# Re-ordering the first weight and input transfers of a fused linear-attention and MLP kernel

## The chip, the cores and the metric

The kernel runs on one core of a Trainium2 chip. The core has five engines that run side by side: TensorE (PE, matrix products and transposes), VectorE (DVE), ScalarE (ACT), GpSimd (POOL) and SyncE (SP, which here only issues DMAs). Sixteen DMA engines move data between memory and the core. The metric is the device time of one execution in microseconds; lower is better.

## The reference

Block-wise linear attention with a decay per head, and behind it a layer norm with a two-layer MLP and a residual:

```python
for b in range(nb):                        # blocks along the sequence, state carried
    intra = einsum('bhic,bhjc->bhij', qb, kb) * Dmask      # Dmask = lam**(i-j), lower triangle
    intra = einsum('bhij,bhjd->bhid', intra, vb)
    inter = einsum('bhid,bhde->bhie', qb * lam_pow, kv_state)
    out[:, :, sl] = intra + inter
    kv_state = lam_block * kv_state + einsum('bhsd,bhse->bhde', kb * rev_pow, vb)
...
xn = (x - mean(x)) / sqrt(var(x) + 1e-06) * g_ln
out = x + maximum(xn @ w_ch1, 0) @ w_ch2
```

q, k and v are 4 x 8 x 768 x 64 (batch, heads, sequence, head size), so x has 3072 rows of 512. w_ch1 is 512 x 2048, w_ch2 2048 x 512. All inputs and the output are float32.

## The kernel before

The 3072 rows are 24 tiles of 128 rows; six tiles make a batch entry, and the attention state runs from tile to tile inside it. For each tile `t` the attention is cut into steps:

- `load_tile(t)` puts three DMAs of 256 KB (k, q, v) on SP's queue. Six buffers of each exist, so tile `t` takes the buffer of tile `t - 6`.
- `p0(t)` issues the load of a later tile and calls `bf_inputs(t)`: POOL makes `kb` (a cast of k, L142), `qb` (q scaled, L144) and `vb` (v scaled, L146), all bf16.
- `p1(t)`: PE transposes `kb` into `tk` and `qb` into `tq`; ACT copies `tk` to `kTp` (two halves), ACT or DVE copies `tq` to `qT`.
- `p2(t)`: PE makes `pk` (the state's increment) and `sc` (the scores); DVE adds the old state (`Stmp`) and masks the scores (`mA`, two halves); POOL multiplies the state by its decay (`Sn`, L185). In the first tile of a batch entry DVE makes `Sn` itself with `lamC`.
- `p3(t)`: PE makes `po` from `mA`, `vb`, `qT` and the state; ACT copies it to `x`; DVE makes the statistics and `xc`.
- `p4(t)`: PE transposes `xc` into `xt`, ACT copies that to `xT` of the tile's group and makes `std`, DVE makes `rstd`.

The MLP works on groups of one to four tiles. For a group of n tiles, `m1(u)` is a unit of first-layer products (`pm`, L254) followed by a ReLU on ACT into `hT`; `m2(i, part)` is a unit of four second-layer products (L267) for tile `i`, and after its fourth part DVE makes `o` and SP stores it. Units with `w1` need the chunk of first-layer weights in question, and `m2(i, part)` needs chunk `part` of `w2`.

The weights come in eight chunks, `load_w1(0..3)` and `load_w2(0..3)`, each issued from POOL's queue with a cast to bf16 (512 KB written). POOL executes its instructions in the order written, so a DMA that POOL issues goes out when POOL has come to it. `load_tile(t, after_pool=True)` ties an SP load to that order: POOL writes one element of the k buffer (L63), and the k load waits for it; SP issues in order too, so all later loads wait behind it.

The order of all engines is the program's order (there is no scheduler). It has three parts: the opening (tiles 0 to 3 with their weights, then the first-layer units of groups 0 and 1), a list `units` with a table `after` that puts attention steps of tiles 4 to 10 between the MLP units of groups 0 to 3, and a loop over the units of the groups from 4 on. That loop spreads the remaining `steps` evenly: at each unit, `rate` is the largest number of steps per unit that any later group still needs (`upto(g)` counts the steps up to the `p4` of the group's last tile), and `pace` adds it up. `round_of(j)` gives the order of steps per round. The opening before, and the group sizes:

```python
sizes = [2, 2, 1, 1, 2, 3, 3, 4, 4, 2]
run((p1, 0), (p2, 0), (p0, 2), (p1, 1), (p3, 0), (p2, 1))
load_w1(0); load_w1(1)
run((p1, 2), (p3, 1)); p0(3); load_w1(2)
run((p2, 2), (p4, 0), (p1, 3), (p3, 2), (p2, 3), (p4, 1))
load_w1(3); load_tile(4, after_pool=True); load_w2(0..3); load_tile(5, after_pool=True)
```

In the text, w1(c) and w2(c) are weight chunks, k4, q4, v4 the inputs of tile 4, and m1a and m1b the first-layer units of groups 0 and 1 in four quarters each (0 to 3).

Of the kernel before, what the change touches and what calls it, by code (L numbers as in the profile page):

```python
# [8 lines left out]
BF16 = mybir.dt.bfloat16  # L9
# [7 lines left out]
def kernel(  # L17
# [11 lines left out]
    nc = tc.nc  # L29
    B, H, S, D = q.shape  # L30
    C = 128
    nb = S // C
    NT = B * nb
    DM = H * D
    DF = moe_w_ch1.shape[1]
    NP = H // 2
# [11 lines left out]
    wk = ctx.enter_context(tc.tile_pool(name="wk", bufs=3))  # L48
# [5 lines left out]
    qkv_in = {}  # L54

    def load_tile(t, after_pool=False):
        b, c = divmod(t, nb)
        got = {}
        for name, src in (("k", k), ("q", q), ("v", v)):
            f = inp.tile([128, H, D], F32, tag=name + "in", name=name + "in")  # L60
            if after_pool:

                nc.gpsimd.memset(f[:, 0, 0:1], 0.0)  # L63
                after_pool = False
            nc.sync.dma_start(f, src[b, :, c * C:(c + 1) * C, :].rearrange("h p d -> p h d"))
            got[name] = f
        qkv_in[t] = got
# [6 lines left out]
    def load_w1(c):  # L74
        nc.gpsimd.dma_start(w1[c], moe_w_ch1[:, c * W1C:(c + 1) * W1C].rearrange("(k p) f -> p k f", p=128))
# [34 lines left out]
    lamC = const.tile([128, NP, 128], F32)  # L110
# [13 lines left out]
    lam_c = const.tile([128, H], F32)  # L124
    nc.scalar.activation(lam_c, lnlam, ACT.Exp, scale=float(C))
    sqrt_first = const.tile([128, 1], F32)
    nc.scalar.activation(sqrt_first, eps_t, ACT.Sqrt)
    lam_cp = lam_c.rearrange("p (a two) -> p a two", two=2)
    nc.vector.tensor_copy(lamC[0:64, :, 0:64], lam_cp[0:64, :, 0:1].to_broadcast([64, NP, 64]))
    nc.vector.tensor_copy(lamC[64:128, :, 64:128], lam_cp[64:128, :, 1:2].to_broadcast([64, NP, 64]))  # L130


    st = {}
# [2 lines left out]
    mv_keep = {}  # L136
    xT_of = {}

    def bf_inputs(t):
        f = qkv_in.pop(t)  # L140
        kb = wk.tile([128, H, D], BF16, tag="kb", bufs=4, name="kb")
        nc.gpsimd.tensor_copy(kb, f["k"])  # L142
        qb = wk.tile([128, H, D], BF16, tag="qb", name="qb")
        nc.gpsimd.tensor_tensor(qb, f["q"], lam_q[:, :, None].to_broadcast([128, H, D]), op=ALU.mult)  # L144
        vb = wk.tile([128, H, D], BF16, tag="vb", bufs=4, name="vb")
        nc.gpsimd.tensor_tensor(vb, f["v"], lam_v[:, :, None].to_broadcast([128, H, D]), op=ALU.mult)  # L146
        st[t] = dict(qb=qb, kb=kb, vb=vb)

    def p1(t):
        s = st[t]  # L150
# [130 lines left out]

        return m1, m2

    sizes = [2, 2, 1, 1, 2, 3, 3, 4, 4, 2]
    groups = [list(range(sum(sizes[:i]), sum(sizes[:i + 1]))) for i in range(len(sizes))]
    assert groups[-1][-1] == NT - 1
    group_of = {t: g for g, ts in enumerate(groups) for t in ts}

    def p0(t):
        if t > 3 and t + 4 < NT:  # L290
            load_tile(t + 4)
        bf_inputs(t)


    def p3_p0(t):
        p3(t)
        if t + 3 < NT:
            p0(t + 3)

    def round_of(j):  # L300
        steps = [(p1, j), (p3_p0, j - 1), (p2, j), (p4, j - 2)]
        return [(f, t) for f, t in steps if t < NT]

    def run(*steps):
        for f, *a in steps:
            f(*a)


    p0(0)
    p0(1)  # L310
    run((p1, 0), (p2, 0), (p0, 2), (p1, 1), (p3, 0), (p2, 1))
    load_w1(0)
    load_w1(1)
    run((p1, 2), (p3, 1))
    p0(3)
    load_w1(2)
    run((p2, 2), (p4, 0), (p1, 3), (p3, 2), (p2, 3), (p4, 1))
    load_w1(3)
    load_tile(4, after_pool=True)
    for c in range(NWC):  # L320
        load_w2(c)
    load_tile(5, after_pool=True)
# [5 lines left out]
    def m1s(f, c):  # L328
        for u in range(c * m1a.count // NWC, (c + 1) * m1a.count // NWC):
            f(u)  # L330
# [3 lines left out]
    m1s(m1a, 1)  # L334
    p4(3)
    m1s(m1a, 2)
    p0(4)
    for c in range(3):
        m1s(m1b, c)
    m1s(m1a, 3)  # L340
# [14 lines left out]

    steps = []
    for j in range(8, NT + 2):
        steps += [s for s in round_of(j) if s not in ((p3_p0, 7), (p4, 7), (p4, 6))]

    def upto(g):  # L360
        return steps.index((p4, groups[g][-1])) + 1 if g < len(groups) else len(steps)
# [47 lines left out]
```

## Time and profile before

| | before |
|---|---|
| median of 3 runs | 247.38 us (247.32 to 247.84) |
| profiled execution, its own time | 246.76 us |
| profiled execution, span from first to last instruction | 245.0 us |
| PE busy | 219.0 us (89% of the span) |
| ACT / DVE / POOL busy | 121.1 / 112.9 / 92.9 us |
| mean granted TensorE clock | 0.986 of full speed |
| DMA traffic | 29.91 MB, mean 122 GB/s |

The profile is one execution on the chip. Each engine has its busy time and the idle time before each instruction, with the instruction or DMA that ended it. A PE that is busy may still run at half clock: the granted clock stands in a row of its own. Lines such as L144 are lines of the kernel before. The 1.76 us between the execution's own time and its span lie outside the instructions; the median of the runs lies 0.62 us above the profiled execution.

### The profile page before, as it was taken

What the parts mean: (1) busy time and instruction counts of PE and PEld (TensorE: products, weight loads), DVE (VectorE), ACT (ScalarE), POOL (GpSimd) and SP (SyncE); (2) the same over time, 40 slices, a digit from 0 to 9 for tenths busy, and PEclk for the clock granted to TensorE, in tenths of its full rate; (3) what the DMA queues carried; (4) which work ended last, traced back from release to release, by engine and by line L of the source; (5) the groups of instructions that cost most, each with busy time, mean ns of one, the idle gap of its engine ahead of it and who ended that gap; (6) DMA issues with size and microseconds to landing.
All of it is one profiled execution on the core that took longest, in us unless ns stands there. A gap on an engine that the chain in (4) does not pass through costs nothing.

```text
span 245.0 us, 4603 instructions
## 1 busy us (share of the span) xinstructions
PE 219.0 (89%) x1856; PEld 142.2 (58%) x1856; DVE 112.9 (46%) x217; ACT 121.1 (49%) x236; POOL 92.9 (38%) x107
## 2 busy tenths in 40 slices
PE   0676894499999897999999999999999999999993
PEld 0565683354587586767755676555555544444851
DVE  3366700033547656798547655475346531122111
ACT  5745775002175366657863487427862247611520
POOL 2779710159500866791566293063322000000000
PEclk9999999689999999999999999999999999999999
DMA  6999999999899999329951960111001120012102
GB/s 127 236 195 146 147 188 196 218 210 210 188 300 208 235 229 219 67 63 237 221 84 43 225 120 4 43 47 43 0 3 43 43 86 3 0 43 88 43 0 86
DMA packets 83012, 29.91 MB, mean 122 GB/s; under 512 B 75568, under 2 KB 79920, under 8 KB 82992
## 3 DMA queue, kind: packets, MB, share of 16 engines
q1 hardware_dynamic: 78624, 25.43, 48.0%
q0 software_dynamic: 4224, 4.19, 10.7%
q8 instruction: 14, 0.23, 0.4%
q14 instruction: 6, 0.05, 0.1%
q10 hardware_dynamic: 144, 0.00, 0.0%
HBM read 27.53 MB, written 6.29 MB: 138 GB/s over the span
## 4 chain that ended last, share of the span: by engine, by line
PE 76%; DMA 8%; ACT 6%; DVE 5%; POOL 2%; issue 2%; DVEq 0%; SPq 0%; ACTq 0%
PE pm L267 33%; PE pm L254 28%; DMA qin<-in_q_dram 7%; PE sc L192 4%; PE po L203 2%; PE xt L230 2%; PE tk L153 2%; PE tq L162 2%; PE po L207 2%; PE pk L177 1%; DVE stats L212 1%; DMA lam_b<-in_lam_dram 1%; ACT kTp L155 1%; ACT x L210 1%; ACT kTp L156 1%
## 5 line engine op out<-in xcount | busy, mean ns | idle before, releaser
L254 PE MATMUL pm<-xT,w 128*128 128x256 bf16 (+3 forms) x640 | 92.6, 298 | 0.7 <-ACT xT L231 0.7
L267 PE MATMUL pm<-w,hT 128*128 128x512 bf16 x384 | 90.5, 381 | 0.0
L257 ACT ACTIVATE hT<-pm 128x512 bf16<-128x512 f32 (+1 forms) x104 | 58.1, 564 | 41.2 <-PE pm L254 40.6
L254 PEld LDWEIGHTS <-w 128*128 128x128 bf16 x640 | 56.9, 99 | 23.8 <-issue 0.8
L267 PEld LDWEIGHTS <-hT 128*128 128x128 bf16 x384 | 36.1, 98 | 36.1 <-issue 0.6
L185 POOL TENSOR_TENSOR Sn<-Stmp,lamC 128x512 bf16<-128x512 f32 x16 | 20.4, 1273 | 69.0 <-DVE Stmp L184 69.0
L212 DVE BATCH_NORM_STATS2 stats<-x 128x6 f32<-128x512 f32 x24 | 16.7, 695 | 46.2 <-ACT x L210 46.1
L278 DVE SCALAR_TENSOR_TENSOR o<-pm,rstd,x 128x512 f32<-128x512 f32 (+1 forms) x25 | 18.0, 725 | 32.7 <-PE pm L267 32.5
L231 ACT COPY xT<-xt 128x512 bf16<-128x512 bf16 x24 | 14.0, 584 | 37.1 <-PE xt L230 37.0
L194 DVE TENSOR_TENSOR mA<-sc,tril 128x512 bf16<-128x512 f32 x48 | 30.7, 680 | 0.0
L144 POOL TENSOR_TENSOR qb<-qin,lam_q 128x512 bf16<-128x512 f32 x24 | 25.8, 1074 | 12.1 <-DMA qin<-in_q_dram 8.6
L146 POOL TENSOR_TENSOR vb<-vin,lam_v 128x512 bf16<-128x512 f32 x24 | 25.5, 1060 | 3.4 <-DMA vin<-in_v_dram 3.0
L155 ACT COPY kTp<-tk 64x512 bf16<-64x512 bf16 x24 | 13.7, 572 | 16.9 <-PE tk L153 16.8
L210 ACT COPY x<-po 128x512 f32<-128x512 f32 x24 | 14.1, 586 | 14.7 <-PE po L207 11.0
L142 POOL CAST kb<-kin 128x512 bf16<-128x512 f32 x24 | 16.6, 690 | 10.8 <-DMA kin<-in_k_dram 10.7
L216 DVE SCALAR_TENSOR_TENSOR xc<-x,mv,g_row 128x512 bf16<-128x512 f32 x24 | 20.2, 840 | 0.9
L162 PE MATMUL tq<-ident,qb 128*128 128x128 bf16 x96 | 10.4, 237 | 11.1 <-POOL qb L144 9.5
L167 DVE COPY qT<-tq 128x512 bf16<-128x512 bf16 x20 | 8.4, 419 | 21.5 <-PE tq L162 21.5
L153 PE MATMUL tk<-ident,kb 128*128 128x128 bf16 x96 | 10.2, 234 | 7.6 <-POOL kb L142 7.6
L192 PE MATMUL sc<-qT,kTp 128*128 128x128 bf16 x192 | 16.4, 234 | 0.3 <-ACT kTp L156 0.2
L192 PEld LDWEIGHTS <-kTp 128*128 128x128 bf16 x192 | 13.5, 106 | 1.3 <-ACT kTp L156 0.4
L156 ACT COPY kTp<-tk 64x512 bf16<-64x512 bf16 x24 | 13.9, 580 | 0.6
(43 smaller groups left out, 127.0 us busy)
## 6 DMA issues: line engine op xcount, KB each, us to landing
kin<-in_k_dram SPq DMA_DIRECT2D x24, 256.0 KB, 4.8
qin<-in_q_dram SPq DMA_DIRECT2D x24, 256.0 KB, 5.1
vin<-in_v_dram SPq DMA_DIRECT2D x24, 256.0 KB, 5.1
out_dram<-o SPq DMA_DIRECT2D x23, 256.0 KB, 2.2
w<-in_moe_w_ch_dram POOLq DMA_DIRECT2D x8, 512.0 KB, 8.7
g_row<-in_moe_g_ln_dram SPq DMA_DIRECT2D x1, 256.0 KB, 4.8
out_dram<-o SPq DMA_DIRECT2D x2, 128.0 KB, 1.7
lam_b<-in_lam_dram ACTq DMA_DIRECT2D x1, 4.0 KB, 3.0
```

What stands on the lines that cost most here:

```text
L142: nc.gpsimd.tensor_copy(kb, f["k"])
L144: nc.gpsimd.tensor_tensor(qb, f["q"], lam_q[:, :, None].to_broadcast([128, H, D]), op=ALU.mult)
L146: nc.gpsimd.tensor_tensor(vb, f["v"], lam_v[:, :, None].to_broadcast([128, H, D]), op=ALU.mult)
L185: nc.gpsimd.tensor_tensor(Sn, tmp, lamC, op=ALU.mult)
L192: nc.tensor.matmul(sc[:, i, :], lhsT=s["kT"][:, h // 2, h % 2, :], rhs=s["qT"][:, h // 2, :], start=(i == 0), stop=(i == H // 2 - 1), skip ...
L194: nc.vector.tensor_tensor(mA[:, half * (H // 2):(half + 1) * (H // 2), :], sc, tril[:, None, :].to_broadcast([128, H // 2, 128]), op=ALU.mult)
L212: nc.vector.bn_stats(stats, x)
L216: nc.vector.scalar_tensor_tensor(xc, in0=x, scalar=mv[:, 0:1], in1=g_row, op0=ALU.subtract, op1=ALU.mult)
L254: nc.tensor.matmul(pm[:, b, :], lhsT=w1[n // W2K][:, kk, (n % W2K) * 128:(n % W2K + 1) * 128], rhs=xT_of[g][:, kk, 0:N], start=(b == 0 and ...
L257: nc.scalar.activation(hT[:, u * NB:(u + 1) * NB, 0:N], pm, ACT.Relu)
L267: nc.tensor.matmul(acc[i], lhsT=hT[:, kk, i * 128:(i + 1) * 128], rhs=w2[kk // W2K][:, kk % W2K, :], start=(kk == 0), stop=(kk == KB - 1))
L278: nc.vector.scalar_tensor_tensor(o[:, sl], in0=a[:, sl], scalar=rstd, in1=x[:, sl], op0=ALU.mult, op1=ALU.add)
```

## The change

Five things are changed.

1. The k casts of tiles 0 and 1 go from POOL to DVE, those of tiles 2 and 3 to ACT; `bf_inputs` is split into `in_k(t, engine)` and `in_qv(t)`. From tile 4 on POOL does all three as before.
2. The two copies that fill `lamC` are written behind the k casts of tiles 0 and 1 on DVE.
3. Weights and the fifth tile's inputs: w1(0) goes ahead of tile 1's `p2`, w1(1) behind tile 3's `in_qv`, and directly behind w1(1) comes the load of tile 4; w1(2) and w1(3) follow tile 3's `p3(2)`. `p0(4)`, that is POOL's work on tile 4, is written ahead of `load_w2` (it stood after the third quarter of m1a). The load of tile 8 moves from `p0(4)` to `p0(5)`.
4. Group sizes: the sixth group has 2 tiles and the last one 3, where it was 3 and 2.
5. In `round_of`, `p4` follows one round after `p1` up to round 11 and two rounds after from round 13 on, where it was two rounds throughout.

```diff
-    lam_cp = lam_c.rearrange("p (a two) -> p a two", two=2)
-    nc.vector.tensor_copy(lamC[0:64, :, 0:64], lam_cp[0:64, :, 0:1].to_broadcast([64, NP, 64]))
-    nc.vector.tensor_copy(lamC[64:128, :, 64:128], lam_cp[64:128, :, 1:2].to_broadcast([64, NP, 64]))
...
-    def bf_inputs(t):
+    def in_k(t, eng):
+        kb = wk.tile([128, H, D], BF16, tag="kb", bufs=4, name="kb")
+        (eng.copy if eng is nc.scalar else eng.tensor_copy)(kb, qkv_in[t]["k"])
+        st[t] = dict(kb=kb)
+
+    def in_qv(t):
         f = qkv_in.pop(t)
-        kb = wk.tile([128, H, D], BF16, tag="kb", bufs=4, name="kb")
-        nc.gpsimd.tensor_copy(kb, f["k"])
...
-        st[t] = dict(qb=qb, kb=kb, vb=vb)
+        st[t].update(qb=qb, vb=vb)
...
-    sizes = [2, 2, 1, 1, 2, 3, 3, 4, 4, 2]
+    sizes = [2, 2, 1, 1, 2, 2, 3, 4, 4, 3]
...
     def p0(t):
-        if t > 3 and t + 4 < NT:
-            load_tile(t + 4)
-        bf_inputs(t)
+        for n in {4: (), 5: (8, 9)}.get(t, (t + 4,)):
+            if n < NT:
+                load_tile(n)
+        in_k(t, nc.gpsimd)
+        in_qv(t)
...
-        steps = [(p1, j), (p3_p0, j - 1), (p2, j), (p4, j - 2)]
+        steps = [(p1, j), (p3_p0, j - 1), (p2, j)]
+        if j <= 11:
+            steps.append((p4, j - 1))
+        elif j > 12:
+            steps.append((p4, j - 2))
...
-    p0(0)
-    p0(1)
-    run((p1, 0), (p2, 0), (p0, 2), (p1, 1), (p3, 0), (p2, 1))
+    for t in range(2):
+        in_k(t, nc.vector)
+        in_qv(t)
+    lam_cp = lam_c.rearrange("p (a two) -> p a two", two=2)
+    nc.vector.tensor_copy(lamC[0:64, :, 0:64], lam_cp[0:64, :, 0:1].to_broadcast([64, NP, 64]))
+    nc.vector.tensor_copy(lamC[64:128, :, 64:128], lam_cp[64:128, :, 1:2].to_broadcast([64, NP, 64]))
+    run((p1, 0), (p2, 0), (p1, 1), (p3, 0))
+    in_k(2, nc.scalar)
+    in_qv(2)
     load_w1(0)
+    run((p2, 1), (p1, 2), (p3, 1))
+    in_k(3, nc.scalar)
+    in_qv(3)
     load_w1(1)
-    run((p1, 2), (p3, 1))
-    p0(3)
+    load_tile(4, after_pool=True)
+    run((p2, 2), (p4, 0), (p1, 3), (p3, 2))
     load_w1(2)
-    run((p2, 2), (p4, 0), (p1, 3), (p3, 2), (p2, 3), (p4, 1))
     load_w1(3)
-    load_tile(4, after_pool=True)
+    run((p2, 3), (p4, 1), (p0, 4))
     for c in range(NWC):
         load_w2(c)
     load_tile(5, after_pool=True)
...
     m1s(m1a, 2)
-    p0(4)
     for c in range(3):
         m1s(m1b, c)
...
-        steps += [s for s in round_of(j) if s not in ((p3_p0, 7), (p4, 7), (p4, 6))]
+        steps += [s for s in round_of(j) if s not in ((p3_p0, 7), (p4, 7))]
```

## The prediction

> **What bounds the kernel now.** I read the page first (busy time per engine, the 40 slices), then the windows, then the chain of waits, and last the timeline of PE, POOL and SP around the places where PE stands still.
>
> ```profile
> PE 219.0 (89%) x1856; PEld 142.2 (58%) x1856; DVE 112.9 (46%) x217; ACT 121.1 (49%) x236; POOL 92.9 (38%) x107
> ...
> PEclk9999999689999999999999999999999999999999
> ```
>
> PE is the engine that is nearly full, and no other reaches half. The granted clock dips in one place only, in the eighth and ninth slice (43 to 55 us). The windows say how the two belong together (columns: window, its length, busy time and instructions of PE, PEld, DVE, ACT, POOL, then granted clock, DMA share and GB/s):
>
> ```profile
> 39.50:46.00 6.50, 0.11 (x3) 0.04 (x2) 0.00 (x0) 1.52 (x3) 1.04 (x1) 0.88 1.22 196
> 46.00:51.00 5.00, 5.00 (x23) 3.26 (x24) 0.42 (x1) 1.19 (x2) 1.04 (x1) 0.50 1.08 213
> ...
> 104.00:225.00 121.00, 121.00 (x929) 69.82 (x928) 62.28 (x119) 63.50 (x129) 37.99 (x39) 1.00 0.30 71
> ```
>
> From 104 to 225 us PE has no gap, at full clock: only removed matmuls could help there, and the change removes none. From 39.5 to 46 PE does nothing, and in the 5 us behind that it runs at half clock. The chain of waits and the timeline name the cause:
>
> ```profile
> 28.69 16.11 DMA qin<-in_q_dram
> ```
>
> ```profile
> 27.87 1.91 PE L254 MATMUL pm<-xT,w 128*128 128x256 bf16 x16
> ...
> 45.96 0.61 PE L162 MATMUL tq<-ident,qb 128*128 128x128 bf16 x4 [6.39 <-POOL qb L144]
> ...
> 46.37 3.62 PE L254 MATMUL pm<-xT,w 128*128 128x256 bf16 x16
> ...
> 49.78 1.80 PE L267 MATMUL pm<-w,hT 128*128 128x512 bf16 x4
> ...
> 57.94 6.21 PE L267 MATMUL pm<-w,hT 128*128 128x512 bf16 x28
> ...
> 71.08 1.03 PE L267 MATMUL pm<-w,hT 128*128 128x512 bf16 x4
> ```
>
> q4, issued at 28.69, lands 16.11 us later; PE waits 6.39 us for the `qb` made of it. Behind the wait the same 16 matmuls take 3.62 us where they took 1.91, and the first four of the second layer 1.80 where they later take 1.03. So the stall costs 6.39 + 1.71 + 0.77 = 8.87 us. Why q4 is late is seen on POOL and in the DMA queues:
>
> ```profile
> 8.66 0.61 POOL L142 CAST kb<-kin 128x512 bf16<-128x512 f32 x1
> ...
> 14.38 1.23 POOL L144 TENSOR_TENSOR qb<-qin,lam_q 128x512 bf16<-128x512 f32 x1 [0.58 <-DMA qin<-in_q_dram]
> 15.57 1.04 POOL L146 TENSOR_TENSOR vb<-vin,lam_v 128x512 bf16<-128x512 f32 x1
> 16.57 1.26 POOL L185 TENSOR_TENSOR Sn<-Stmp,lamC 128x512 bf16<-128x512 f32 x1
> 17.78 1.68 POOL L75 DMA_DIRECT2D w<-in_moe_w_ch_dram  x2
> 19.45 1.12 POOL L142 CAST kb<-kin 128x512 bf16<-128x512 f32 x1
> ...
> 21.55 1.03 POOL L146 TENSOR_TENSOR vb<-vin,lam_v 128x512 bf16<-128x512 f32 x1
> ...
> 28.13 0.12 POOL L63 MEMSET kin<- 128x1 f32 x1
> 28.17 2.97 POOL L78 DMA_DIRECT2D w<-in_moe_w_ch_dram  x4
> ```
>
> ```profile
> q0 software_dynamic: 1256, 1.24, 91.1%
> q1 hardware_dynamic: 1255, 0.31, 29.9%
> ```
>
> The second fence is the DMA view of 36 to 44 us (packets, MB, share): q0 carries the weights, q1 the inputs. The queues get one packet each in turn, but a weight packet is about 1 KB and an input packet 256 bytes: 155 GB/s for the weights, 39 for the inputs. w2(0..3) goes out at 28.17, together with tile 4's loads, and holds them back until it is done.
>
> **The change part by part.** *Removed: the stall.* POOL in the new order: `qb` of tile 2 waits for its q as before and `vb` ends at 16.6, w1(0) takes 0.8 (17.4), `Sn` 1.26 (18.7), `qb` and `vb` of tile 3 2.0 (from the cast's end at 20.57 to 22.58; so 20.8, and the cast's 1.12 is gone), w1(1) 0.8, the memset: k4, q4 and v4 go out at about 21.9 instead of 28.27. In front of them on the engines are three w1 chunks only. Prices of the queues, from the DMA views of 22 to 26 us (weights alone) and 52 to 58 us (inputs alone), and from the landings of w1, w2 and v:
>
> ```profile
> DMA packets 818, 0.82 MB, mean 205 GB/s; under 512 B 31, under 2 KB 817, under 8 KB 817
> ...
> DMA packets 5146, 1.30 MB, mean 217 GB/s; under 512 B 5145, under 2 KB 5145, under 8 KB 5145
> ...
> L75 POOL DMA_DIRECT2D w<-in_moe_w_ch_dram x4: 753/803/937, 17.8 to 27.3; - x4
> ...
> DMA to landing us min/median/max: 5.5/6.1/8.0
> ...
> L78 POOL DMA_DIRECT2D w<-in_moe_w_ch_dram x4: 747/765/780, 28.2 to 30.4; - x4
> ...
> DMA to landing us min/median/max: 9.4/13.9/17.9
> ...
> 29.31 3.56 SPq L65 DMA_DIRECT2D vin<-in_v_dram  x1
> ...
> DMA to landing us min/median/max: 4.1/5.1/19.5
> ```
>
> A chunk of 0.524 MB takes 2.56 us of queue alone and lands 5.5 us after its issue at best, so about 2 us pass before its first byte moves. w1(1..3), 1.57 MB, begin at 22.8; inputs join at about 24; the remaining 1.3 MB at 155 GB/s last until 32.5. By then the inputs have 0.33 of their 0.786 MB; the rest at 217 GB/s takes 2.1 us: v4 lands at about 35. PE reaches tile 4's transposes at 39.57 (45.96 less 6.39), so the wait and its half clock go: **-8.87**. Without this cover (q4 after 38.4) each us of lateness would be one on PE.
>
> *Added: w2 behind v4.* POOL now makes `kb`, `qb` and `vb` of tile 4 before it issues w2, so w2(0) goes out at v4's landing plus one `vb`, 36.1, against 28.17: 8 us later. It lands at 41.6 at best. The four landed 3.57 us apart before ((30.4 + 17.9) - (28.2 + 9.4) over three), which already holds inputs beside them, as k5 would be again from about 42; so w2(3) lands at 52.3. PE comes to the first unit of the second layer at 49.78 - 6.39 - 1.71 = 41.7, no wait. Its tenth unit, the first with w2(3), began at 57.94 plus two units of 0.86 = 59.7; less 8.87 that is 50.8. So PE waits 1.5 us in all for w2: **+1.5**. Bounds: 0 if the chunks come 2.56 apart, 7 if v4 needs the 19.5 us that it needed before; I take the row of w2 itself.
>
> [...]
>
> *k casts off POOL, `lamC` copies behind them: 0.* PE's wait of 1.53 us for `kb` of tile 3 looks like the prize, but this is what follows it:
>
> ```profile
> 18.98 1.12 DVE L216 SCALAR_TENSOR_TENSOR xc<-x,mv,g_row 128x512 bf16<-128x512 f32 x1
> ...
> 20.62 0.61 PE L153 MATMUL tk<-ident,kb 128*128 128x128 bf16 x4 [1.53 <-POOL kb L142]
> 20.63 1.27 DVE L194 TENSOR_TENSOR mA<-sc,tril 128x512 bf16<-128x512 f32 x2
> ...
> 22.03 0.64 PE L203 MATMUL po<-vb,mA 128*128 128x64 bf16 x8
> ```
>
> tile 2's `po` needs both halves of `mA`, done at 21.9 on DVE, whatever tile 3's `kb` does. The serial chain x, statistics, `xc`, `Stmp`, `mA`, `po` paces the opening; with `kb` early, PE idles before `po` instead. DVE's second cast must wait for tile 1's k (POOL's cast of it started at 8.66) and holds the `lamC` copies and tile 0's `mA` back by about one cast, 0.6, which is in time for tile 2, whose q comes at 14.38. ACT's casts I price at POOL's 1.12 at most: tile 2's starts when its k lands, as POOL's did, and tile 3's stands ahead of the copy of tile 0's `xt`, which only the first-layer units need. Bounds for the opening: -0.5 (an `xc` without its 1.12) to +1.7 (the first 16 first-layer matmuls at half clock, if PE's new pause lets it stay cold). I take 0, as either way PE meets w2(3) at 52.3 again: a loss up to 1.5 is covered by the wait above, and a gain lengthens it.
>
> *Group sizes and `round_of`.* The multiset of sizes is the same, so PE's products cost the same; the end (two half stores of the last tile) is the same too. What changes is how tightly the steps of tiles 8 to 13 are packed. Counted by the loop's own arithmetic, the fifth group's 16 units carried 17 steps, now 13, and never two behind one unit:
>
> ```profile
> 82.31 0.39 PE L207 MATMUL po<-Sn,qT 128*128 128x128 bf16 x4
> ...
> 85.28 0.40 PE L230 MATMUL xt<-ident,xc 128*128 128x128 bf16 x4 [0.86 <-DVE xc L216]
> ...
> 93.16 0.39 PE L177 MATMUL pk<-vb,kb 128*128 128x128 bf16 x4
> ...
> 93.83 0.39 PE L153 MATMUL tk<-ident,kb 128*128 128x128 bf16 x4
> 95.85 0.38 PE L162 MATMUL tq<-ident,qb 128*128 128x128 bf16 x4 [1.64 <-DVE Stmp L184]
> ```
>
> Here `p2(9)` and `p1(10)` follow each other directly, `tq` needs the PSUM buffer that `Stmp` must free, and PE waits 1.64: **-1.64**. But `p4` now comes a round earlier: from `po`'s end to the earliest `xt` lie 85.28 - 82.70 = 2.58 us, and in the new list two units (1.74) and a `p2` (0.67, or 0.45 without `pk`) lie between for tiles 9 and 10: waits of 0.2 and 0.4: **+0.6** (bounds 0 to 2, if ACT's ReLU comes first each time). Tile 8 has three units and no wait.
>
> *Tile 5 and later.* k5 goes out behind w2 at 39.3, begins near 41.3 and gets 39 GB/s until 51.8; the 0.38 MB that tile 5 then lacks take 1.7 at 217: v5 lands near 54. `p1(5)` stands behind the fourteenth unit, at 52.3 plus five units, 56.6: its q, a third of 0.786 MB earlier, has 2 us of cover after its `qb`. Later loads go out in the order they had. 0, bounds 0 to 1.
>
> Sum: 245.0 - 8.87 + 1.5 + 0 - 1.64 + 0.6 = 236.6 us of span; with the 1.76 us around it 238.4 beside 246.76, and with the 0.62 by which the median lies above the profiled execution, **239.0 us**.
>
> **The rivals.** *w2 in time.* If the inputs beside it are few, chunks come 2.56 apart: w2(3) at 49.3, before the 50.8, and the 1.5 goes: 237.5. The 155 against 39 GB/s speaks against it. [...]
>
> *w2 late, PE cold again.* If the inputs are starved as long as before (19.5 us), v4 lands at 41.4, w2(0) at 48.0 and w2(3) at 58.7: 6.4 more, 245.4. PE would stand 6 us and run at half clock behind it, but that is mostly covered by the waits for the next chunks. Against it: the queue in front is three chunks, not five. [...]
>
> *Slower.* The same place, one mechanism: w2 leaves POOL only after v4. To lose, w2(3) must land 8.9 us after 52.3 (239.0 to 247.9), so v4 22 us after its issue or later, more than any input needed in this trace.
>
> *No effect.* If tile 4's loads were not earlier at all: their issue hangs on POOL's memset alone, which moves ahead of two w1 chunks, all of w2 and two `Sn`. I see nothing for it.
>
> **How the numbers follow.** Forecast, w2(3) waited for by 0.5 to 3 us: 0.57 (its own range 237.8 to 240.5). w2 in time or an opening that also helps: 0.22 (236.3 to 237.8). w2 late: 0.15 (240.5 to 246). Same: 0.02, slower: 0.04 (both the last mechanism). Range 236.5 to 242.0, which leaves out the far end of the late case. A measurement of this kernel tells 0.2% (0.5 us) from no change; faster beyond that 0.94.
>
> **What would show it.** Right: k4 issued near 22, no PE gap of 6 us near 40, granted clock 1.0 from 40 to 55, w2's first issue near 36, PE gaps of 1 to 2 us by w2 between 42 and 53, `tq` without the 1.64, small gaps of `xt` behind `xc`. Wrong: a PE gap of over 3 us before a second-layer unit with half clock after it; `qb` of tile 5 late; or first-layer units near 25 us stretched to half speed.

## The result, and the profile after

The changed kernel takes 239.94 us (median of four runs, 238.34 to 240.41); the kernel before, timed beside it, 247.35. The ratio is 0.9693, 95% interval 0.964 to 0.9745: faster, by 7.4 us. The forecast was 239.0 in a range of 236.5 to 242.0. The profiled execution is the longest of the four, 240.41 us with a span of 238.7; forecast were 238.4 and 236.6. So the median lies 0.9 us from the forecast and the span 2.1. All the same, the forecast had one step wrong and one term missing; part of the nearness is luck. A few executions in this study run at a low mean granted clock (one of the first experiment's at 0.77, 296.92 us); the ratios are of the others.

First the page: busy time and granted clock of the kernel after.

```profile
PE 217.7 (91%) x1856; PEld 141.1 (59%) x1856; DVE 115.6 (48%) x219; ACT 122.5 (51%) x238; POOL 89.9 (38%) x103
...
PEclk9998599999999999999999999999999999999998
```

PE has as many matmuls as before. The dip of the clock near 50 us is gone, but there is a new one in the fifth slice (24 to 30 us). The windows of the kernel after show both (same columns as before):

```profile
24.00:27.00 3.00, 2.33 (x21) 2.04 (x19) 2.15 (x4) 1.37 (x3) 0.91 (x2) 0.50 1.24 231
27.00:30.00 3.00, 3.00 (x30) 2.38 (x29) 1.35 (x4) 0.98 (x2) 1.82 (x2) 0.68 1.25 207
39.50:46.00 6.50, 6.50 (x67) 5.53 (x66) 0.74 (x2) 4.54 (x8) 0.00 (x0) 1.00 1.22 196
46.00:51.00 5.00, 5.00 (x35) 2.52 (x33) 2.77 (x6) 0.59 (x1) 1.70 (x2) 1.00 1.21 198
```

From 39.5 to 51, where PE stood for nearly 6.5 us and then ran at half clock, it is now full at clock 1.0. The timeline of PE, first two lines of the kernel before that the comparison needs, then the kernel after (line numbers are always those of the kernel shown):

```profile
25.16 1.91 PE L254 MATMUL pm<-xT,w 128*128 128x256 bf16 x16 [0.67 <-ACT xT L231]
...
30.45 8.90 PE L254 MATMUL pm<-xT,w 128*128 128x256 bf16 x80
```

```profile
22.71 0.40 PE L203 MATMUL po<-vb,mA 128*128 128x64 bf16 x4 [2.36 <-DVE mA L194]
...
26.51 3.08 PE L254 MATMUL pm<-xT,w 128*128 128x256 bf16 x16 [0.67 <-ACT xT L231]
...
33.17 0.40 PE L230 MATMUL xt<-ident,xc 128*128 128x128 bf16 x4 [1.16 <-DVE xc L216]
33.40 8.90 PE L254 MATMUL pm<-xT,w 128*128 128x256 bf16 x80
...
42.36 0.39 PE L162 MATMUL tq<-ident,qb 128*128 128x128 bf16 x4
...
44.33 1.03 PE L267 MATMUL pm<-w,hT 128*128 128x512 bf16 x4
...
52.01 6.21 PE L267 MATMUL pm<-w,hT 128*128 128x512 bf16 x28
```

`tq` of tile 4 (42.36) follows without a wait, and no second-layer unit waits for w2. But the opening is late. The first sixteen first-layer matmuls began at 25.16 and took 1.91; now they begin at 26.51 and take 3.08. The third quarter of m1a began at 30.45; now at 33.40, 2.95 us later: 1.35 by the late start, 1.17 by the half clock, 0.72 by the longer wait for `xc` of tile 3 (1.16 in place of 0.44), less 0.29 by which the second quarter followed the first sooner. The first second-layer unit gains 49.78 - 44.33 = 5.45 us. The first unit with w2(3) stands two units of 0.86 behind 52.01, at 53.7, where it was at 59.7: a gain of 5.9, which is 8.87 less 2.95.

Two fences of the timeline of all engines in the kernel after show what makes the opening late:

```profile
18.86 1.05 POOL L144 TENSOR_TENSOR qb<-qin,lam_q 128x512 bf16<-128x512 f32 x1
...
18.97 2.49 DVE L216 SCALAR_TENSOR_TENSOR xc<-x,mv,g_row 128x512 bf16<-128x512 f32 x1
...
19.86 1.04 POOL L146 TENSOR_TENSOR vb<-vin,lam_v 128x512 bf16<-128x512 f32 x1
```

```profile
31.52 1.04 POOL L144 TENSOR_TENSOR qb<-qin,lam_q 128x512 bf16<-128x512 f32 x1 [2.53 <-DMA qin<-in_q_dram]
...
31.67 1.44 DVE L216 SCALAR_TENSOR_TENSOR xc<-x,mv,g_row 128x512 bf16<-128x512 f32 x1
```

`xc` of tile 1 starts at 18.97, as before (18.98), but takes 2.49 us in place of 1.12: it ends 0.56 us behind the end of POOL's `vb` (20.90). In DVE's order `Stmp` and `mA` of tile 2 come behind it, and `po` waits for `mA`. `xc` of tile 3, beside `qb` of tile 4, takes 1.44 and makes the wait of 1.16. The loads, in the timeline and in the group of w2's issues of the kernel after:

```profile
21.79 0.37 SPq L65 DMA_DIRECT2D kin<-in_k_dram  x1
...
36.08 3.04 POOL L78 DMA_DIRECT2D w<-in_moe_w_ch_dram  x4
```

```profile
L78 POOL DMA_DIRECT2D w<-in_moe_w_ch_dram x4: 750/766/812, 36.1 to 38.4; - x4
...
DMA to landing us min/median/max: 6.6/10.4/14.3
```

w2(0) lands at 36.1 + 6.6 = 42.7, w2(3) at 38.4 + 14.3 = 52.7. The pacing, in PE's timeline of the kernel after:

```profile
102.66 0.40 PE L230 MATMUL xt<-ident,xc 128*128 128x128 bf16 x4 [0.54 <-DVE xc L216]
...
109.62 0.38 PE L162 MATMUL tq<-ident,qb 128*128 128x128 bf16 x4 [0.40 <-DVE Sn L181]
```

The 1.64 us of `tq` behind `Stmp` are gone; 0.54 and 0.40 have come.

### The profile page after: what moved, and what is told of

The parts are those of the page before. It is cut to its first block, busy times and chain, and to the rows that moved or that the text cites. A ratio compares the mean times of both kernels' runs of the same rounds, so it can differ in the third digit from the quotient of the medians.

```text
span 238.7 us, 4607 instructions
## 1 busy us (share of the span) xinstructions
PE 217.7 (91%) x1856; PEld 141.1 (59%) x1856; DVE 115.6 (48%) x219; ACT 122.5 (51%) x238; POOL 89.9 (38%) x103
## 2 busy tenths in 40 slices
DMA packets 83013, 29.91 MB, mean 125 GB/s; under 512 B 75569, under 2 KB 79921, under 8 KB 82993
## 4 chain that ended last, share of the span: by engine, by line
PE 80%; DVE 9%; ACT 7%; issue 2%; POOL 0%; DVEq 0%; POOLq 0%
PE pm L267 33%; PE pm L254 32%; PE sc L192 4%; DVE xc L216 3%; PE xt L230 3%; DVE stats L212 2%; PE po L203 2%; PE po L207 2%; ACT x L210 2%; PE tk L153 2%; PE tq L162 2%; PE pk L177 1%; DVE mA L194 1%; ACT kTp L155 1%; ACT hT L257 1%
## 5 line engine op out<-in xcount | busy, mean ns | idle before, releaser
L144 POOL TENSOR_TENSOR qb<-qin,lam_q 128x512 bf16<-128x512 f32 x24 | 25.1, 1045 | 17.1 <-DMA qin<-in_q_dram 15.3
L146 POOL TENSOR_TENSOR vb<-vin,lam_v 128x512 bf16<-128x512 f32 x24 | 26.3, 1096 | 4.6 <-DMA vin<-in_v_dram 2.5
L216 DVE SCALAR_TENSOR_TENSOR xc<-x,mv,g_row 128x512 bf16<-128x512 f32 x24 | 21.8, 909 | 0.9
L155 ACT COPY kTp<-tk 64x512 bf16<-64x512 bf16 x24 | 13.7, 572 | 14.4 <-PE tk L153 14.3
L138 POOL CAST kb<-kin 128x512 bf16<-128x512 f32 x20 | 12.7, 634 | 3.2 <-DMA kin<-in_k_dram 3.1
L162 PE MATMUL tq<-ident,qb 128*128 128x128 bf16 x96 | 9.9, 230 | 3.9 <-POOL qb L144 3.5
```

The costliest lines, as they stand in the source:

```text
L216: nc.vector.scalar_tensor_tensor(xc, in0=x, scalar=mv[:, 0:1], in1=g_row, op0=ALU.subtract, op1=ALU.mult)
```

## The experiments

Ratios are to the kernel before on the same chip, with their 95% intervals. A ratio of 0.001 is 0.25 us.

**The parts alone.** First the order of the DMAs without the rest: tile 4's loads and POOL's work on tile 4 are moved, and with them the load of tile 8 (from `p0(4)` to `p0(5)`, not shown); w1(0) and w1(1) stay where they were, the casts stay on POOL, the sizes and rounds as before.

```diff
     p0(3)
+    load_tile(4, after_pool=True)
     load_w1(2)
     run((p2, 2), (p4, 0), (p1, 3), (p3, 2), (p2, 3), (p4, 1))
     load_w1(3)
-    load_tile(4, after_pool=True)
+    p0(4)
     for c in range(NWC):
         load_w2(c)
...
     m1s(m1a, 2)
-    p0(4)
```

> The kernel before with one part of the change: tile 4's loads released behind tile 3's vb, POOL's work on tile 4 ahead of w2 (and the load of tile 8 moved with it); casts, group sizes and rounds as before. Theory (port): the opening of the changed kernel loses 2.95 us because DVE's xc of tile 1 is blocked while POOL makes qb and vb of tile 3; with the old POOL order xc stays near 1.1 us, the first first-layer unit starts near 25.2, and the whole 8.9 us of stall and half clock is won: w2(3) lands near 51, no wait over 1 us for w2, span 236 to 237, more than the whole change won. Rival (the order of DMAs itself costs the opening its time, by transfers that collide): the first unit starts after 26, span 238 to 239.

Measured: 241.56 us, ratio 0.9789 (0.9759 to 0.9819). The same kernel a second time:

> The kernel dma_order_alone once more, for a profile at full clock. Theory (tile 4's loads, released ahead of w1(2), delay w1(2) and with v4 the whole of w2): a wait of 1 to 2 us for w1(2) before the third quarter of m1a, w2(3) landing near 54 and a wait for it, ratio 0.977 to 0.981, span near 240. xc of tile 1 near 1.1 us, first first-layer unit near 25.2, as in the kernel before.

Measured: 241.67 us, ratio 0.9792 (0.9766 to 0.9818). So this part alone makes 5.2 us of the 7.4 (0.021 of 247). The first expectation was right on `xc` and wrong on the time: it had a span of 236 to 237 and w2(3) near 51, and the span is 240.4, with w2(3) at 55.0. Its timeline, DVE and then PE:

```profile
19.43 1.13 DVE L216 SCALAR_TENSOR_TENSOR xc<-x,mv,g_row 128x512 bf16<-128x512 f32 x1
```

```profile
25.83 1.91 PE L254 MATMUL pm<-xT,w 128*128 128x256 bf16 x16 [0.67 <-ACT xT L231]
...
30.68 0.40 PE L230 MATMUL xt<-ident,xc 128*128 128x128 bf16 x4 [0.44 <-DVE xc L216]
32.67 8.91 PE L254 MATMUL pm<-xT,w 128*128 128x256 bf16 x80 [1.58 <-DMA w<-in_moe_w_ch_dram]
...
44.51 1.04 PE L267 MATMUL pm<-w,hT 128*128 128x512 bf16 x4 [0.74 <-DMA w<-in_moe_w_ch_dram]
...
51.67 1.02 PE L267 MATMUL pm<-w,hT 128*128 128x512 bf16 x4 [0.69 <-DMA w<-in_moe_w_ch_dram]
...
55.08 4.48 PE L267 MATMUL pm<-w,hT 128*128 128x512 bf16 x20 [0.44 <-DMA w<-in_moe_w_ch_dram]
```

With the casts left on POOL `xc` takes 1.13, and the first sixteen first-layer matmuls 1.91. In place of a late opening come waits for weights: 1.58 us for w1(2), which now goes out behind the release of tile 4's inputs (PE waits for it until 32.67; in the kernel before it had landed at 29.25), and 0.74 + 0.69 + 0.44 = 1.87 for w2. The wait for w2 is the term of +1.5 of the prediction; the wait for w1(2) the prediction does not have. -8.87 + 1.58 + 1.87 and 0.67 of a later start of m1a come to -4.75; the span went from 245.0 to 240.4.

Then the group sizes and `round_of` alone, as in the diff of the change.

> The kernel before with the new group sizes and the new round order only. Theory: the 1.64 us gap of tq behind Stmp goes, gaps of xt behind xc of 0.5 to 1 us come in its place: span 244.0 to 244.6, ratio near 0.997. Rival (pacing is worth as much as forecast, 1.0 us, or more, since most of the win is here): 243 or less. The stall near 40 us stays at 6.4 in both.

Measured: 245.7 us, ratio 0.9968 (0.9949 to 0.9986). PE's timeline of this kernel:

```profile
45.96 0.61 PE L162 MATMUL tq<-ident,qb 128*128 128x128 bf16 x4 [5.73 <-POOL qb L144]
...
108.02 0.40 PE L230 MATMUL xt<-ident,xc 128*128 128x128 bf16 x4 [0.54 <-DVE xc L216]
...
114.98 0.38 PE L162 MATMUL tq<-ident,qb 128*128 128x128 bf16 x4 [0.40 <-DVE Sn L181]
```

The stall stays, ending at the same 45.96; the same two small waits have taken the place of 1.64. This part is worth 0.8 us (0.3 to 1.3). The two parts together make 6.0 us; the rest, 0.5 to 1.4 us by the two ratios of the changed kernel (0.9693 above, 0.9738 further down), belongs to the casts and the new places of w1(0) and w1(1), and was not split further.

**What holds `xc`.** The theory: an `xc` with both its inputs in SBUF can't run beside a POOL instruction that has begun before it. ("Port" in the expectations is a name for this theory; what the two engines share no run here shows.) The rival: not `xc`, but the later w1(1) and PE's own pause make the opening late. Three edits of the changed kernel.

```diff
     in_k(3, nc.scalar)
-    in_qv(3)
     load_w1(1)
+    in_qv(3)
```

> The changed kernel with w1(1) issued ahead of tile 3's qb and vb instead of behind them. Theory (port): xc of tile 1 runs beside a DMA issue, takes 0.75 to 1.1 instead of 2.49, PE's 2.36 us pause shrinks to about 1, the first first-layer unit starts near 25 and at full clock; PE then meets w2(3) (landing near 52.7): a wait of 1 to 2 us appears before the tenth second-layer unit, and the net win is about 1 us, span near 237.7. [...]

Measured: 238.6 us, ratio 0.9689 (0.966 to 0.9718), span 236.9. On `xc` I was wrong (timeline, POOL and DVE):

```profile
19.02 0.80 POOL L75 DMA_DIRECT2D w<-in_moe_w_ch_dram  x1
19.85 1.06 POOL L144 TENSOR_TENSOR qb<-qin,lam_q 128x512 bf16<-128x512 f32 x1
20.85 1.50 POOL L146 TENSOR_TENSOR vb<-vin,lam_v 128x512 bf16<-128x512 f32 x1
```

```profile
19.27 2.19 DVE L216 SCALAR_TENSOR_TENSOR xc<-x,mv,g_row 128x512 bf16<-128x512 f32 x1
```

POOL now issues a DMA when `xc` starts, and `xc` is held all the same: through the issue, then through `qb`, and it ends 0.55 behind `qb`. This time `vb` gives way (1.50 in place of 1.04). `mA` and m1a are no earlier for it: the first quarter starts at 26.52, where it was 26.51. What this trace gains it gains elsewhere: the first sixteen matmuls took 2.40 in place of 3.08; `qb` of tile 4 starts at 28.97 in place of 31.52, so that `xc` of tile 3 is clear of it (0.75); and w2 goes out at 35.26 in place of 36.08. By the ratio the kernel can't be told from the changed one (0.9693 and, further down, 0.9738).

Next `xc` of tiles 1 and 3 reads its first input from PSUM, where it is computed, and not from its copy in SBUF.

```diff
-        nc.vector.scalar_tensor_tensor(xc, in0=x, ...)
+        xin = po.rearrange("p h d -> p (h d)") if t in (1, 3) else x
+        nc.vector.scalar_tensor_tensor(xc, in0=xin, ...)
```

> The changed kernel; xc of tiles 1 and 3 reads po from PSUM instead of its copy x in SBUF, so that DVE has one SBUF input; POOL's order is untouched. Theory (port): xc of tile 1 takes 0.7 to 0.9 although POOL's qb and vb run beside it, xc of tile 3 falls from 1.44 to the same, first first-layer unit near 25, net win about 1 us as w2 takes over. Rival (xc is slow because POOL or the SBUF is busy in any case): xc stays over 1.4 and the span at 238 to 239.

Measured: 239.72 us, ratio 0.9728 (0.9699 to 0.9758), span 238.0, clock 1.0. The timeline (DVE, POOL, then PE):

```profile
18.98 0.75 DVE L217 SCALAR_TENSOR_TENSOR xc<-po,mv,g_row 128x512 bf16<-128x512 f32 x1
```

```profile
19.03 1.05 POOL L144 TENSOR_TENSOR qb<-qin,lam_q 128x512 bf16<-128x512 f32 x1
```

```profile
24.78 1.91 PE L255 MATMUL pm<-xT,w 128*128 128x256 bf16 x16 [0.67 <-ACT xT L232]
...
31.62 8.91 PE L255 MATMUL pm<-xT,w 128*128 128x256 bf16 x80 [1.57 <-DMA w<-in_moe_w_ch_dram]
...
53.19 4.48 PE L268 MATMUL pm<-w,hT 128*128 128x512 bf16 x20 [0.37 <-DMA w<-in_moe_w_ch_dram]
```

The same `xc` at the same place beside the same `qb` takes 0.75 in place of 2.49, and m1a starts 1.7 us earlier, its first sixteen matmuls at 1.91. So what holds `xc` here is that both its inputs lie in SBUF: 2.49 us with both there, 0.75 with one in PSUM. The order of the starts, as the theory has it, does not decide it: in the changed kernel `vb` began at 19.86 and went ahead of the `xc` that had waited since 18.97. And yet the kernel is hardly faster, where about 1 us had been expected: it now waits for w1(1) (0.37), for w1(2) (1.57) and in three places for w2 (0.37 + 0.27 + 0.37 = 1.0). What the opening gains the transfers take back.

The control, and the changed kernel once more on its chip: the four casts of k go back to POOL, in the changed order.

```diff
-        in_k(t, nc.vector)          # tiles 0, 1; nc.scalar for tiles 2, 3
+        in_k(t, nc.gpsimd)          # all four
```

> The changed kernel unaltered, on the same chip as the next three, for comparison. Ratio to before near 0.969; xc of tile 1 over 2 us in its profile if the port theory holds, as nothing in it is random.

> The changed kernel with all k casts of tiles 0 to 3 back on POOL (the lamC copies then run early again); DMA order, sizes and rounds as changed. Theory (port, and transfers set the opening's end): the casts are worth 0 to 0.7 us: POOL's chain up to the memset is one cast longer for tile 3, tile 4 and w2 go out 0.6 to 1 us later, xc of tile 1 is still blocked by POOL (1.2 to 2.5 us). Span 238.5 to 239.5. Rival (the casts carry part of the win): 240.5 or more.

Measured: the changed kernel 240.33 us, 0.9738 (0.9701 to 0.9776), with `xc` of tile 1 at 2.37 and m1a's first quarter at 3.04; casts back on POOL 240.73, 0.9752 (0.9716 to 0.9788). The timeline of the latter:

```profile
19.34 2.91 DVE L216 SCALAR_TENSOR_TENSOR xc<-x,mv,g_row 128x512 bf16<-128x512 f32 x1
...
20.66 1.03 POOL L146 TENSOR_TENSOR vb<-vin,lam_v 128x512 bf16<-128x512 f32 x1
```

With the cast, `qb` and `vb` all behind one another on POOL, `xc` is held longer still (2.91, again ending 0.56 behind `vb`). So it is not the move of the casts that makes the collision, but the order in which POOL's work now stands beside `xc`. In the kernel before that was a DMA issue and behind it a cast, and there the cast gave way (1.12 us where a free one takes 0.61). `qb` and `vb` did not here, though `vb` did with w1(1) ahead of `qb`. What decides which POOL instruction gives way stays open. The casts are worth 0.35 us by the ratios, which the intervals can't tell from nothing.

**What the transfers take back.** In the changed kernel w2 waits for `vb` of tile 4, and from 35.5 to 37.5 us the DMA engines move nothing at all (0 packets, 0 GB/s). With `xc` of tiles 1 and 3 from PSUM, w2 goes out between `qb` and `vb` of tile 4:

```diff
-    run((p2, 3), (p4, 1), (p0, 4))
-    for c in range(NWC): load_w2(c)
+    run((p2, 3), (p4, 1))
+    in_k(4, nc.gpsimd)
+    in_qv(4, between=lambda: [load_w2(c) for c in range(NWC)])   # ahead of vb
```

> xc of tiles 1 and 3 from PSUM as before, and w2 issued between qb and vb of tile 4 instead of behind vb. Theory (the opening's gain is eaten by transfers): the DMA hole near 36 us goes, w2(3) lands near 51 instead of 53.15, the four waits for w2 (1.0 us) go, those for w1(1) and w1(2) (1.9 us) stay: span about 237.0. Rival (the win of the faster opening is lost somewhere else): still 238.

Measured: 239.36 us, ratio 0.9695 (0.9658 to 0.9733), span 238.5 where 237.0 was expected. The waits for w2 are gone, the one for w1(2) is not (timeline of PE, then the windows of this kernel):

```profile
31.66 10.57 PE L257 MATMUL pm<-xT,w 128*128 128x256 bf16 x80 [1.30 <-DMA w<-in_moe_w_ch_dram]
```

```profile
32.00:34.00 2.00, 2.00 (x15) 1.54 (x13) 0.00 (x0) 0.60 (x1) 2.00 (x3) 0.65 1.21 196
34.00:36.00 2.00, 2.00 (x11) 1.45 (x10) 0.00 (x0) 0.60 (x1) 2.00 (x4) 0.50 1.14 189
```

Here the clock fell behind the wait (0.65, then 0.50), and 80 matmuls took 10.57 us, not 8.90: 1.67 more.

Then also w1(1) ahead of `qb` of tile 3, and w1(2) ahead of tile 4's loads:

```diff
+    load_w1(1)
     in_qv(3)
-    load_w1(1)
+    load_w1(2)
     load_tile(4, after_pool=True)
     run((p2, 2), (p4, 0), (p1, 3), (p3, 2))
-    load_w1(2)
     load_w1(3)
```

> As the run with w2 ahead of vb, and w1(1) ahead of tile 3's qb and w1(2) ahead of tile 4's loads. Theory: the waits for w1(1) and w1(2) go too, third quarter of m1a near 30, tile 4's q lands near 33 (in time for 39), second-layer units start near 41.5 and w2(3), landing near 50, is waited for by less than 0.5: span 235 to 236, ratio 0.958 to 0.962. Rival (w1(2) was late for another reason than tile 4's loads): the 1.6 us wait before the third quarter of m1a stays.

Measured: 237.62 us, ratio 0.9652 (0.9618 to 0.9685). w1(2) is there when PE needs it (the third quarter of m1a starts at 29.91 without a wait for it), and the span is 235.9, as expected; 0.29 + 0.43 us of waits for w2 remain. Against `xc` from PSUM alone (0.9728) that is what the transfers had taken back. On this kernel two more, run together: `xc` of all tiles from PSUM, and on top of that w2 issued right behind `kb` of tile 4, ahead of `qb` and `vb`.

> As psum_xc_weights_first, but xc of every tile reads po from PSUM, so that no xc can be blocked by POOL. Theory (port): every xc takes 0.75, PE's later waits for xc (0.5, 0.86 and 0.54 us) shrink to about 0.2 to 0.5 each, span about 235.0 to 235.5, 0.5 to 0.9 below the kernel it is made from. Rival (po held longer by DVE stops the next tile's p3, as there is one po buffer): new gaps at po, span 236 or more.

> As all_xc_from_psum, with w2 issued directly behind kb of tile 4, ahead of its qb and vb. Theory (transfers): k4, q4 and v4 land within 2 us of each other here, so w2 goes out 1.3 us sooner without starving them; the two waits for w2 (0.7 us) go, qb of tile 4 is ready at 37.5, in time for PE at 38.6: span 0.5 to 0.7 below all_xc_from_psum. Rival: q4 or v4 is starved by w2 and PE waits before tile 4's transposes: span above it.

Measured: 237.74, ratio 0.9636 (0.9605 to 0.9667), and 236.75, ratio 0.9599 (0.9573 to 0.9626). The first can't be told from tiles 1 and 3 alone (0.9652); its profiled span is 235.1 against 235.9, and all 24 `xc` take 0.75. The second is the best version of this study, faster than the changed kernel by 1.0% to 1.4% by the ratios (against 0.9693 and 0.9738). Why it beats the first is not shown: w2 was expected 1.3 us sooner, but it goes out at 34.01 against 34.04 in the two profiles, and in neither has PE a wait for weights left. PE in the second:

```profile
30.10 8.90 PE L257 MATMUL pm<-xT,w 128*128 128x256 bf16 x80
...
48.48 6.21 PE L270 MATMUL pm<-w,hT 128*128 128x512 bf16 x28
```

Last, the kernel before with nothing but the mended DMA order: w1(2) ahead of tile 4's loads, w2 between `qb` and `vb` of tile 4. Casts on POOL, pacing and `xc` as before; the load of tile 8 and the old `p0(4)` as in the first experiment (not shown).

```diff
     load_w1(2)
+    load_tile(4, after_pool=True)
     run((p2, 2), (p4, 0), (p1, 3), (p3, 2), (p2, 3), (p4, 1))
     load_w1(3)
-    load_tile(4, after_pool=True)
-    for c in range(NWC): load_w2(c)
+    bf_inputs(4, between=lambda: [load_w2(c) for c in range(NWC)])
```

> The kernel before with the DMA order alone, but w1(2) issued ahead of tile 4's loads and w2 between qb and vb of tile 4. Casts, sizes and rounds as before. Theory: with w1(2) in time (landing near 30) and w2(3) near 50 nothing of the 8.9 us is given back: no PE gap over 0.7 us between 25 and 55, span 236 to 237, ratio 0.962 to 0.968, more than the whole change wins. Rival (the old opening with its POOL casts cannot feed this order): waits for q4 or w2 of over 1 us, span 238 or more.

Measured: 238.29 us, ratio 0.9654 (0.9627 to 0.9681), against 0.9792 on the same chip for the order as the change has it. Its timeline of PE:

```profile
31.36 8.90 PE L256 MATMUL pm<-xT,w 128*128 128x256 bf16 x80
...
42.28 1.03 PE L269 MATMUL pm<-w,hT 128*128 128x512 bf16 x4
...
49.67 6.21 PE L269 MATMUL pm<-w,hT 128*128 128x512 bf16 x28
```

No wait for w1(2), none for w2. w1(2) and w2 moved by a place each are together worth 3.4 us (0.0138 of the ratio), four times the pacing. So this one re-ordering is at least as fast as the whole change (0.9693 and 0.9738).

## Why the prediction was right, and where it was wrong

*The stall, -8.87: right.* k4 went out at 21.79 (forecast 21.9), v4 landed at 35.02 (35; though w1(3) took until 34.61, not 32.5, and a lone chunk's 5.5 less 2.56 leaves 2.9 us, not 2, outside its transfer), w2 went out at 36.08 (36.1), w2(3) landed at 52.70 (52.3). The dip of the clock and the slow first unit of the second layer went with the stall. The rivals that hang on a late v4 (245.4, and slower) did not occur. Most of the gain is this, as the parts alone show: 5.2 us by the DMA order, 0.8 by the pacing.

*The opening, 0: the step that failed.* It measured +2.95, beyond its upper bound of 1.7. I took POOL's work between 18 and 21 us from the kernel before and did not ask what DVE does beside it. Moving w1(1) behind `qb` and `vb` put both next to `xc`, with the cast or without it (and without the cast `qb` alone holds it, 2.19, when w1(1) goes ahead); 1.37 us more of `xc` delay `mA`, `po` and m1a, 16 matmuls take 3.08 us at a clock of 0.50 to 0.68, and tile 3's `xc` meets `qb` of tile 4. The half clock, 1.17 of the 2.95, is the least certain part. In this trace it comes with PE's pause of 2.36 us. But with the casts back on POOL the 16 matmuls took 2.04 behind a pause of 2.15 (mean clock of that execution 0.996), and in the second trace of the changed kernel the clock had fallen ahead of the pause: 0.79 from 12 to 18 us, 0.50 from 18 to 27. One of the four executions had a span of 236.6, as forecast, and no trace shows it, so how much of the 2.95 is in every execution is not known. "Done at 21.9 on DVE" for `mA` was 23.25. The row that could have told was in the prediction's own fence: an `xc` of 1.12 us, where most of the 24 take 0.75. The bound of 1.7 held the half clock, and not the collision. The line "first-layer units near 25 us stretched to half speed", given as a sign of error, is what came.

*w2, +1.5: right as a mechanism, not there in the sum.* The prediction said that a loss of the opening of up to 1.5 would be covered by the wait for w2(3). That is what happened: PE comes to w2(3)'s unit at 50.8 + 2.95 = 53.7, and the chunk landed at 52.7. Where the opening is not late the wait is there: 1.87 us with the DMA order alone, 1.0 with `xc` from PSUM. Of the 2.95 the wait would have hidden 1.5; what is left, 1.45, is most of the 2.1 us by which the span was missed. So the case that was given 0.57 (w2(3) waited for) was not the one that ran, though the time fell into it: that is luck, a missing wait paying for half of a late opening.

*w1(2): a term that was missing.* Tile 4's inputs, let out ahead of w1(2), delay it: it landed at 29.25 before and at 31.29 after, and with the DMA order alone PE waited for it until 32.67. The prediction counted w1 as what delays the inputs and never asked the reverse. The changed kernel is too late to notice; the versions whose opening is on time wait 1.3 to 1.6 us for it, until w1(2) goes first.

*Pacing, -1.04: about right.* The 1.64 went. Of the small waits forecast for `xt` (0.2 for tile 9, 0.4 for tile 10) the second came, with 0.54, and one of 0.40 for `tq` behind `Sn` that I had not seen. PE's gaps in that stretch fell by 0.76; by the time of this part alone it is 0.8. (Before, the loop puts 18 steps behind the fifth group's units, not 17; nothing in the sum hangs on it.)

*Tile 5, 0: right.* Its `tq` follows without a wait.

*The clock behind a short wait: not the same each time.* The sum lets PE go on at full clock behind 1.5 us of waits, as it did before behind the 1.64 of `tq` (0.38 us for the four matmuls, clock 1.00 from 95.8 to 98). A wait of 1.58 with 0.44 shortly before it kept the clock in one kernel (80 matmuls in 8.91), one of 1.30 with 0.54 before it lost it in another (10.57).

## What to carry to other kernels

Before an instruction of POOL is moved or dropped, look at what DVE runs at that time: an operation that takes longer than its shortest twin may be held, as `xc` was here (2.49 us against 0.75), by what POOL does next as well (`vb`, begun 0.89 us after it); one input left in PSUM freed it here (0.75). When loads are reordered, list for each transfer that is overtaken when PE needs it: here, of the 8.87 us of a stall removed, waits for the next transfers in line took 3.45 back with the DMA order alone. A term of 0 in a sum deserves the same bounds as the large one, and a wait that follows absorbs only part of its error: here it would have hidden 1.5 of 2.95 us.

## What the runs showed of the hardware

`xc` was held not only by POOL's arithmetic, but by a DMA issue of POOL that had begun before it. In the kernel before it ended 0.64 us behind the two issues (17.78 + 1.68, and 18.98 + 1.12). With the DMA order alone it is again 0.64 behind:

```profile
18.23 1.69 POOL L75 DMA_DIRECT2D w<-in_moe_w_ch_dram  x2
```

(19.92, against 19.43 + 1.13 = 20.56.) Behind `vb` or `qb` it ended 0.55 to 0.56 later in three kernels (0.56 in the changed one, 0.55 with w1(1) ahead of `qb`, 0.56 with the casts back on POOL). An issue that came behind the `vb` that held `xc` did not hold it further in the two of them that have one: `xc` ended at 21.46 beside the issue of 20.84 to 21.65 in the changed kernel, and at 22.25 beside that of 21.65 to 22.46 with the casts back.

The granted clock fell behind short pauses, and not each time. Behind 1.30 + 0.54 us of idling within some 2.3 us it was 0.50 (80 matmuls in 10.57 us); behind 1.58 + 0.44 within 2.4 us the same 80 took 8.91. What tells the two apart no run here shows.

The cast of k (128x512, f32 to bf16) takes 0.43 us on DVE and 0.62 on ACT, against 0.61 on POOL when nothing holds it. I had priced ACT's at 1.12, which was a POOL cast held by `xc`.
